# The last 64 columns of x's second half: transposing loads in place of plain loads and identity matmuls

## The chip, the cores and the metric

The kernel runs on one core of a Trainium2 chip. A core has a matrix engine (PE, TensorE), a vector engine (DVE), a scalar engine (ACT), a general engine (POOL, GpSimd) and SyncE (SP), which here only issues DMAs. Each engine runs its own instructions in order, and semaphores tie them together. Matmul results land in PSUM and are copied to SBUF by ACT or DVE. The metric is device time in microseconds of one execution.

## The reference

Two independent blocks are computed, and their outputs are put side by side. B = 1, S = 2048 positions, D = 576 channels, bf16.

```python
# A: dilated sliding-window attention, 32 heads of 18
qkv = x @ wqkv
logits[s, w] = q[s] . k[s - 2 w] * scale        # w = 0..7, masked below 0
o = softmax(logits) @ v[s - 2 w];  a = o @ wo
# B: a long convolution with gates
kv = (short 4-tap convolution of k along s) * v
y = irfft(rfft(kv) * rfft(ssm_k)) + kv * ssm_D   # causal, length S
b = q_B * y
out = concat([a, b], -1)
```

## The kernel before

**x.** The projections need x transposed: channels on partitions, positions along the row. 576 channels are four blocks of 128 and a tail of 64. `xT(kb, t0, n)` is a block's view in the large SBUF tile `xw`; `x5(jj)` is the tail of one half jj of the positions, 128 x 512, whose lower 64 partitions hold the half's first 512 positions and whose upper 64 the other 512. The first half of x is loaded as it lies (`load_x`) and transposed by PE. The second half comes by `turn_x(h)`, once for each 512 positions: a transposing DMA brings the first 512 columns straight into `xT`, and a plain DMA brings the last 64 columns as they lie into `xnat`, a view of the tile `Ks`. `transpose_tail(1)` then multiplies those 2 x 4 pieces of 128 positions with the identity on PE (L490) and copies the 128 x 512 result out of PSUM on ACT (L492).

**SP's queue.** The loads are issued from SP in program order: x, weights, k's segment 0, v's segment 0, k's segment 1, `turn_x(0)`, `turn_x(1)` (L250, L251), v's segment 1 (L219, L220), and later, as buffers come free, k's segments 2 and 3 (L210, L213), v's segments 2 and 3, and the filter's transposing loads (L227).

**The first stage** (to about 56 us). DVE runs `taps(i)`, the 4-tap convolution of the segments i = 0 to 3, each of 512 positions: multiplications L577, additions L581, and the product with v, L597. Beside it PE projects q and k. `project(comp, jj)` makes units for column blocks of 128, two halves of 512 positions each: four matmuls a half with `xT` (L378), the 64-row tails with `x5` (L389), and an ACT copy of the 128 x 1024 result (L414). L382 and L395 are the same for the last 64 columns of q or k. After each `taps(i)`, two `mirror(i, n)` units fold a segment on PE (L606) with two ACT copies (L609). `table_i` transposes sine tables on PE (L455) with two ACT copies (L459). `fold_filter(m)` folds a filter segment (L673, ACT L676).

**Order.** It is written out by hand. `units` is a list of closures for PE and ACT; `until()` runs as many of them as the next number in PLACES says (2, 14 and 13 after the first three segments' taps). Mirrors and fold units are inserted into what is left of the list at the places of AT (1, 5 and 19), where a mirror is not put between the two halves of a projection. `need(label)` runs all units up to the last one with that label; after the last segment `need("fold3")` empties the list. `early` runs a unit and advances the planner's clock for PE. PSUM tiles have two tags, "A" and "B", with two buffers each; projections, table_i and fold_filter use "A", the mirrors and `transpose_tail` use "B".

**Behind it**, `logits(hh)` multiplies q and shifted k on DVE (L832) and sums over the channels on PE (L847), two products at a time; then come softmax, the weighted sums, the output projection, the spectra (L627, L776) and the inverse transform.

Of the kernel before, what the change touches and what calls it, by code (L numbers as in the profile page):

```python
# [11 lines left out]
ACT = mybir.ActivationFunctionType  # L12
ALU = mybir.AluOpType
FP32 = mybir.dt.float32
# [39 lines left out]
def view(t, offset, dims):  # L54

    return bass.AP(tensor=t.tensor, offset=t.offset + offset, ap=[list(t.ap[0])] + [list(d) for d in dims])
# [3 lines left out]
def kernel(  # L60
# [13 lines left out]
    nc = tc.nc  # L74
# [4 lines left out]
    xf = A_x.flatten_outer_dims()  # L79
# [29 lines left out]
    pp = ctx.enter_context(tc.tile_pool(name="pp", bufs=2, space=PSUM))  # L109
# [32 lines left out]
    def x5(jj):  # L142
        return view(xw, HB * (3 + 3 * jj) + 4096, [[1, 512]])
# [39 lines left out]
    xnat = view(Ks, 4 * HB, [[HB, 4], [D, 4], [1, D]])  # L183
# [14 lines left out]
    def load_k(i):  # L198

        eng = nc.sync  # L200
        kj = sp1.tile([128, 7, D], BF16, name="kj", bufs=2)
        r0 = BL * i
        low = [(0, 64)]
        if i == 0:
            nc.gpsimd.memset(kj[0:1, 0:3, :], 0.0)
            nc.gpsimd.dma_start(kj[0:1, 3:7, :], kf[0:4, :].unsqueeze(0))
            low = [(1, 49), (49, 64)]
        for a, b in ((3, 7), (0, 3)) if i == 0 else ((0, 7),):
            for p0, p1 in low:
                eng.dma_start(kj[2 * p0:2 * p1:2, a:b], bass.AP(  # L210
                    tensor=kf.tensor, offset=kf.offset + (r0 + 4 * p0 - 3 + a) * D,
                    ap=[[4 * D, p1 - p0], [D, b - a], [1, D]]))
            eng.dma_start(kj[1:128:2, a:b], bass.AP(tensor=kf.tensor, offset=kf.offset + (r0 + 256 + 3 - a) * D,  # L213
                                                    ap=[[4 * D, 64], [-D, b - a], [1, D]]))
        kjs.append(kj)
# [24 lines left out]
    ident = main.tile([128, 128], BF16, name="ident")  # L240
# [6 lines left out]
    def turn_x(h):  # L247

        r0 = 1024 + 512 * h
        nc.sync.dma_start(xnat[:, 2 + h, :, 512:576], xf[r0:r0 + 512, 512:576].rearrange("(sb p) c -> p sb c", p=128))  # L250
        nc.sync.dma_start_transpose(view(xw, 6 * HB + 512 * h, [[1024, 4], [1, 512]]), xf[r0:r0 + 512, 0:512])  # L251

    load_k(0)
    load_w(nc.sync, 1)
    load_v(0)
    load_k(1)
    turn_x(0)
    turn_x(1)
    load_v(1)

# [61 lines left out]
    units = deque()  # L322
# [160 lines left out]
        f()  # L483
        clk["P"] += us

    def transpose_tail(jj):
        pt = pp.tile([128, 512], FP32, name="ps_x", tag="B")
        for jp in range(2):
            for sb in range(4):
                nc.tensor.matmul(pt[64 * jp:64 * jp + 64, 128 * sb:128 * sb + 128], xnat[:, 2 * jj + jp, sb, 512:576],  # L490
                                 ident[:], start=True, stop=True, tile_position=(0, 64 * jp))
        nc.scalar.activation(x5(jj), pt[:], ACT.Copy)  # L492

    def project_first(jp, ct0):

        ps = bank2("ps_proj", "A")
        for e in range(2):
            c0 = 128 * (ct0 + e)
            for kb in range(4):
                nc.tensor.matmul(ps[:, e, :], wq(kb, 0, c0, 128), xT(kb, 512 * jp, 512), start=(kb == 0), stop=False)  # L500
        for e in range(2):
            nc.tensor.matmul(ps[:, e, :], wq(4, 0, 128 * (ct0 + e), 128)[64 * jp:64 * jp + 64],
                             x5(0)[64 * jp:64 * jp + 64], start=False, stop=True, tile_position=(64 * jp, 0))
        nc.scalar.activation(view(q, S * ct0 + 512 * jp, [[S, 2], [1, 512]]), ps[:], ACT.Copy)
# [40 lines left out]
    for jj in range(2):  # L545
        if jj:
            project(0, jj)
        project(1, jj)
        if jj == 0:
            units.append((0.43, partial(early, partial(transpose_tail, 1), 0.43), "x"))  # L550
    project(0, 2)
    project(1, 2)

# [792 lines left out]
```

## Time and profile before

| | |
|---|---|
| median of 3 runs | 212.2 us (212.09 to 212.56) |
| the profiled execution | 212.5 us, of which the traced span is 210.8 |
| granted TensorE clock | 0.998 |
| PE busy | 200.1 us (95%) |
| DVE busy | 193.1 us (92%) |
| ACT busy | 150.5 us (71%) |
| POOL busy | 74.0 us (35%) |
| DMA | 39.66 MB in 35,396 packets |

An engine's busy time is a sum over stages that are limited by different things. A row of the timeline gives the start and the length of a group of like instructions; a bracket at its end gives the time for which the engine had been idle and what ended that. A row marked SPq is SP's time for issuing a DMA, not the transfer; the time to landing is told apart.

### The profile page before, as it was taken

The page shows a single profiled execution, that of the slowest core. Times are in us where ns is not written, and L with a number is a line of the kernel's source. Part 1 is how long each engine was busy: PE and PEld are TensorE (multiplying, and loading weights), DVE is VectorE, ACT ScalarE, POOL GpSimd, SP SyncE. Part 2 cuts the span into 40 slices and gives each one's busy share as a digit, 9 for nine tenths or more (in the row PEclk, how much of TensorE's full clock was granted, in tenths as well). Part 3 has the DMA queues.
Part 4 walks back from the last instruction along what each step waited for, and adds up shares of the span by engine and source line. Part 5 has one row for each costly group of instructions (what it writes and reads, how often), then busy time and mean ns, then how long its engine had stood idle before and what let it go on. Part 6 is the DMA issues. An engine that isn't in the chain of part 4 may idle for free.

```text
span 210.8 us, 5106 instructions
## 1 busy us (share of the span) xinstructions
PE 200.1 (95%) x2114; PEld 110.7 (53%) x2122; DVE 193.1 (92%) x146; ACT 150.5 (71%) x218; POOL 74.0 (35%) x111
## 2 busy tenths in 40 slices
PE   7999999999999999899999999999989999999891
PEld 2443443344554656564354666656555666666460
DVE  7989999999999999858889999999999849999981
ACT  3799988657684989986369788855666796775540
POOL 8999993001195516320175000002029004033000
PEclk9999999999999999999999999999999999999999
DMA  6999998999639336999999997587559995985133
GB/s 201 303 328 231 266 342 280 170 192 182 151 75 122 48 40 87 180 181 171 235 225 238 194 234 159 105 208 185 153 223 255 239 322 110 214 243 182 28 113 111
DMA packets 35396, 39.66 MB, mean 188 GB/s; under 512 B 17619, under 2 KB 29007, under 8 KB 35374
## 3 DMA queue, kind: packets, MB, share of 16 engines
q1 hardware_dynamic: 26812, 24.88, 47.2%
q0 software_dynamic: 6096, 11.96, 30.4%
q10 hardware_dynamic: 2466, 2.51, 3.5%
q8 instruction: 16, 0.26, 0.5%
q14 instruction: 6, 0.05, 0.1%
HBM read 13.11 MB, written 4.72 MB: 85 GB/s over the span
## 4 chain that ended last, share of the span: by engine, by line
PE 80%; ACT 10%; DVE 5%; issue 2%; DVEq 0%; ACTq 0%
PE ps_proj L378 16%; PE ps_z L1126 9%; PE ps_wo L1029 8%; PE ps_acc L973 7%; PE ps_inv L1158 7%; PE ps_fx L776 6%; PE ps_log L847 4%; PE ps_proj L500 3%; PE ps_fk L627 3%; PE ps_proj L382 3%; PE ps_proj L389 3%; ACT Ks L695 3%; PE ps_rev L673 2%; PE ps_fk L628 1%; ACT qk L977 1%
## 5 line engine op out<-in xcount | busy, mean ns | idle before, releaser
L378 PE MATMUL ps_proj<-xw 128*128 128x512 bf16 x153 | 37.4, 380 | 0.6 <-issue 0.3
L832 DVE TENSOR_TENSOR av<-qk 128x4096 bf16<-128x4096 bf16 (+1 forms) x16 | 31.7, 2013 | 2.8 <-PE ps_log L847 2.8
L378 PEld LDWEIGHTS <-xw 128*128 128x128 bf16 x160 | 14.0, 97 | 20.5 <-issue 6.2
L1099 DVE TENSOR_TENSOR qk<-xw,Ks 128x2304 bf16<-128x2304 bf16 x14 | 18.5, 1355 | 2.5 <-PE ps_inv L1158 2.4
L1139 ACT ACTIVATE av<-ps_z 128x768 bf16<-128x768 f32 x20 | 15.3, 808 | 6.2 <-PE ps_z L1126 6.2
L414 ACT ACTIVATE qk<-ps_proj 128x1024 bf16<-128x1024 f32 x14 | 14.3, 1023 | 7.6 <-PE ps_proj L389 3.3
L695 ACT ACTIVATE Ks<-ps_fk 128x576 bf16<-128x576 f32 x32 | 18.6, 717 | 1.3 <-PE ps_fk L628 1.3
L577 DVE TENSOR_TENSOR tB<-kj,skb 128x4608 bf16<-128x4608 bf16 (+1 forms) x8 | 19.3, 2417 | 0.1
L778 ACT ACTIVATE xw<-ps_fx 128x576 bf16<-128x576 f32 x32 | 18.4, 666 | 0.0
L776 PE MATMUL ps_fx<-xw,TB 128*128 128x288 bf16 x128 | 18.0, 286 | 0.2
L1055 POOL DMA_DIRECT2D Ks<-Ks x3 | 3.7, 1218 | 41.1 <-PE ps_wo L1029 28.7
L1029 PE MATMUL ps_wo<-qk 128*128 128x288 bf16 x128 | 17.8, 287 | 0.0
L627 PE MATMUL ps_fk<-Ks,TB 128*128 128x384 bf16 x62 | 16.9, 326 | 0.8 <-ACT Ks L695 0.7
L414 ACT ACTIVATE v<-ps_proj 128x1024 bf16<-128x1024 f32 x9 | 9.3, 1029 | 9.3 <-PE ps_proj L378 4.3
L973 PE MATMUL ps_acc<-av,ident 64*64 64x512 bf16 x160 | 15.3, 377 | 0.0
L628 PE MATMUL ps_fk<-Ks,TB 128*128 128x192 bf16 x62 | 15.2, 245 | 0.0
L776 PEld LDWEIGHTS <-TB 128*128 128x128 bf16 x128 | 12.0, 97 | 6.0 <-issue 2.9
L1029 PEld LDWEIGHTS <-qk 128*128 128x128 bf16 x128 | 11.6, 98 | 5.6 <-issue 3.0
L1158 PE MATMUL ps_inv<-av,TI 128*128 128x288 bf16 (+1 forms) x96 | 13.6, 293 | 0.6 <-ACT av L1139 0.6
L1161 ACT ACTIVATE v<-ps_inv 128x576 bf16<-128x576 f32 (+1 forms) x14 | 9.5, 677 | 6.3 <-PE ps_inv L1158 6.3
L977 ACT ACTIVATE qk<-ps_acc 128x1024 bf16<-128x1024 f32 x8 | 8.2, 1024 | 8.0 <-PE ps_acc L973 8.0
L956 DVE TENSOR_TENSOR av<-Ks,v 128x4096 bf16<-128x4096 bf16 x6 | 13.6, 2286 | 0.2 <-PE ps_acc L973 0.2
(199 smaller groups left out, 471.3 us busy)
## 6 DMA issues: line engine op xcount, KB each, us to landing
Ks<-Ks POOLq DMA_DIRECT2D x9, 576.0 KB, 7.1
TB<-av SPq DMA_DIRECT2D x12, 256.0 KB, 5.5
kj<-in_B_k_dram SPq DMA_DIRECT2D x6, 504.0 KB, 6.1
vt<-in_B_v_dram SPq DMA_DIRECT2D x8, 288.0 KB, 5.2
Ks<-av SPq DMA_DIRECT2D x8, 256.0 KB, 5.5
Ks<-Ks SPq DMA_DIRECT2D x3, 576.0 KB, 6.1
Ks<-in_A_x_dram SPq DMA_DIRECT2D x2, 576.0 KB, 5.2
xw<-in_A_wqkv_dram SPq DMA_DIRECT2D x2, 576.0 KB, 5.9
```

Of the source, the lines that this page charges most:

```text
L378: nc.tensor.matmul(ps[:, jp, :], wq(kb, comp, 128 * ct, 128), xT(kb, 1024 * jj + 512 * jp, 512), **se)
L414: nc.scalar.activation(view(t, o + pad + 1024 * jj, [[512, 2], [1, 512]]), ps[:], ACT.Copy)
L577: dve(2304 * n, lambda: nc.vector.tensor_tensor(to, view(kj, row * D, [[D, n], [D, 4], [1, D]]), view(skb, row * D, [[D, n], [0, 4], [1, D ...
L627: nc.tensor.matmul(o[:, 0:2], w, rhs[:, 0:2], start=start, stop=stop)
L695: nc.scalar.activation(view(Ks, k_at(m, cs ^ (m & 1)) + 96 * gi, [[768, 3], [384, 2], [1, 96]]), acc3(ps), ACT.Copy, scale=(PSG, MSG)[cs][ ...
L776: nc.tensor.matmul(ps[:, pm, 0:HD], TX[:, 2 * pm + c, 128 * gi:128 * gi + 128], kv[:, 2 * c + pm, HD * h:HD * h + HD], start=(c == 0), sto ...
L832: return P, at, step, dve(1024 * nj, lambda: nc.vector.tensor_tensor(view(P, at, [[step, 4], [256, nj], [1, 256]]), view(t, o + 256 * hh, ...
L973: nc.tensor.matmul(acc[64 * o:64 * o + 64, h, :], ident[64 * h:64 * h + 64, 64 * h:64 * h + 64], view(P, 256 * u, [[2048, 2], [1, 256]])[6 ...
L1029: nc.tensor.matmul(ps[:, r, 0:HD], oT(hh, 2 * c + r, t)[:, o:o + 128], wo[:, t // 2, t % 2, HD * h:HD * h + HD], start=(t == 0 and h == 0) ...
L1099: r = dve(3 * QTR, lambda: nc.vector.tensor_tensor(pr, view(xw, HB * XG[i] + QTR * t, [[HB, 3], [1, QTR]]), view(Ks, k_at(j - i, 0) + QTR ...
L1126: nc.tensor.matmul(view(acc[r], 512 * h, [[192, 2], [96, 2], [1, 96]])[o:o + 64], w[64 * h:64 * h + 64, 64 * h:64 * h + 64], pr[64 * h:64 ...
L1158: nc.tensor.matmul(ps[:, c, 0:n], TI[:, sl, pm, 128 * c:128 * c + 128], Y(j, pm)[:, sl, c0:c0 + n], start=(pm == 0 and sl == 0), stop=(sl ...
```

## The change

`turn_x(h)` no longer loads the last 64 columns as they lie. After the transposing load of the first 512 columns, a second transposing load brings the last 64 straight into the 64 partitions of `x5(1)` that belong to these 512 positions. `transpose_tail` goes, and with it its unit in the list. The numbers in PLACES and AT stay.

```diff
     def turn_x(h):
         r0 = 1024 + 512 * h
-        nc.sync.dma_start(xnat[:, 2 + h, :, 512:576], xf[r0:r0 + 512, 512:576].rearrange("(sb p) c -> p sb c", p=128))
         nc.sync.dma_start_transpose(view(xw, 6 * HB + 512 * h, [[1024, 4], [1, 512]]), xf[r0:r0 + 512, 0:512])
+        nc.sync.dma_start_transpose(x5(1)[64 * h:64 * h + 64], xf[r0:r0 + 512, 512:576])
...
-    def transpose_tail(jj):
-        pt = pp.tile([128, 512], FP32, name="ps_x", tag="B")
-        for jp in range(2):
-            for sb in range(4):
-                nc.tensor.matmul(pt[64 * jp:64 * jp + 64, 128 * sb:128 * sb + 128], xnat[:, 2 * jj + jp, sb, 512:576],
-                                 ident[:], start=True, stop=True, tile_position=(0, 64 * jp))
-        nc.scalar.activation(x5(jj), pt[:], ACT.Copy)
...
         project(1, jj)
-        if jj == 0:
-            units.append((0.43, partial(early, partial(transpose_tail, 1), 0.43), "x"))
```

## The prediction

> **What bounds the kernel now.** I read the page first, then the timeline of the stretch around the edit, then the waits of the vector engine, then the timeline down to where engines meet again. The first columns of a timeline row are start and length in us.
>
> ```profile
> PE 200.1 (95%) x2114; PEld 110.7 (53%) x2122; DVE 193.1 (92%) x146; ACT 150.5 (71%) x218; POOL 74.0 (35%) x111
> PE 80%; ACT 10%; DVE 5%; issue 2%; DVEq 0%; ACTq 0%
> ```
>
> PE and DVE are both nearly full, so the chain, 80% PE, names only the one that was last. What 0.4 us of PE work is worth depends on which engine sets the pace between the edit (near 30 us) and the next meeting of the two. The edit's own stretch:
>
> ```profile
> 28.62 1.04 PE L378 MATMUL ps_proj<-xw 128*128 128x512 bf16 x4
> 28.73 1.08 ACT L459 ACTIVATE TI<-ps_ti 128x512 bf16<-128x512 f32 x2 [0.36 <-PE ps_ti L455]
> 29.58 0.42 PE L490 MATMUL ps_x<-ident,Ks 128*64 128x128 bf16 x8
> 29.70 1.03 ACT L414 ACTIVATE qk<-ps_proj 128x1024 bf16<-128x1024 f32 x1
> 29.94 1.90 PE L378 MATMUL ps_proj<-xw 128*128 128x512 bf16 x7
> 30.61 0.61 ACT L492 ACTIVATE xw<-ps_x 128x512 bf16<-128x512 f32 x1
> 31.77 0.60 PE L389 MATMUL ps_proj<-xw 64*128 64x512 bf16 x4
> ```
>
> L490 and L492 are the work that goes. And this is what DVE waited for in the first 75 us, all of it:
>
> ```profile
> DVE xw L161 <- PEq L1330: 0.9, 1, 0.9
> DVE xw L577 <- DMA kj<-in_B_k_dram: 0.7, 1, 0.7
> DVE tB L173 <- issue: 0.3, 1, 0.3
> ...
> 11.88 1.36 DVE L577 TENSOR_TENSOR xw<-kj,skb 128x2304 bf16<-128x2304 bf16 x1 [0.72 <-DMA kj<-in_B_k_dram]
> ```
>
> After 11.88 us DVE waits for nobody; it runs the taps and then the logits products on its own clock. Where PE meets it:
>
> ```profile
> 63.87 2.27 DVE L832 TENSOR_TENSOR av<-qk 128x4096 bf16<-128x4096 bf16 x1
> ...
> 65.75 0.62 PE L847 MATMUL ps_log<-v,E 128*32 128x512 bf16 x8
> ...
> 66.20 0.60 PE L847 MATMUL ps_log<-av,E 128*32 128x512 bf16 x8
> ```
>
> The second half of this L847 group reads the product that DVE ends at 63.87 + 2.27 = 66.14. It starts at 66.20, 0.06 later, which is a semaphore's way: PE has no slack against DVE here. Anything that PE gains before 66.20 beyond those 0.06 us becomes waiting.
>
> **Removed from PE and ACT.** Eight matmuls at L490 and one copy at L492. PE's step from 29.58 to 29.94 is 0.36 us, the most that can leave the chain. But the projection behind it can't simply move up by 0.36. It takes one of the two buffers of tag "A". One holds the tile that ACT empties from 29.70 to 30.73; so at 29.94 it is in the other, table_i's, which ACT (L459) empties until 28.73 + 1.08 = 29.81. PE follows such a release by 0.06 (66.14 to 66.20), so it can start at 29.87: a gain of 0.07 us; the rest of L490's time only covered ACT's copy. L492's 0.61 us on ACT falls in a stretch where ACT then idles: its next instruction comes at 32.26, after 1.04 us of waiting (row below). It brings nothing by itself.
>
> **What moves.** The unit that disappears was one of those which until() pops by hand-written counts (2, 14, 13). With one fewer, the second count takes one projection half more, and mirror units, inserted at fixed places among what is left, move:
> - Segment 1's first mirror goes from in front of the third pair of projection halves to behind it. Its input is ready at 33.40 (32.04 + 1.36 of L597), its output is read only in the x spectrum, behind the logits; nothing waits on it.
> - ACT's table load at 33.31 is issued one projection's copy later. ACT waits about 1 us between such copies (1.04 in the row), so I cost it at nothing; without that cover it would be 1.28 us on ACT, not on PE, which has a second buffer.
> - Segment 2's second mirror goes from 50.6 us to behind the last key projection, right ahead of fold_filter(3). This one is tight.
>
> ```profile
> 32.26 1.02 ACT L414 ACTIVATE qk<-ps_proj 128x1024 bf16<-128x1024 f32 x1 [1.04 <-PE ps_proj L389]
> 33.31 1.28 ACT L739 ACT_TABLE_LOAD   x1
> ...
> 32.04 1.36 DVE L597 TENSOR_TENSOR xw<-xw,vt 128x2304 bf16<-128x2304 bf16 x1
> 33.32 2.55 DVE L577 TENSOR_TENSOR tB<-kj,skb 128x4608 bf16<-128x4608 bf16 x1
> ...
> 51.49 1.92 PE L382 MATMUL ps_proj<-xw 128*64 128x512 bf16 x16
> 51.58 1.19 ACT L609 ACTIVATE xw<-ps_fold 128x576 bf16<-128x576 f32 x2
> 53.45 1.02 ACT L414 ACTIVATE qk<-ps_proj 128x1024 bf16<-128x1024 f32 x1 [0.68 <-PE ps_proj L382]
> 54.53 0.41 PE L673 MATMUL ps_rev<-Ks,flip 128*128 128x288 bf16 x2 [0.28 <-ACT qk L414]
> 54.97 1.19 ACT L676 ACTIVATE Ks<-ps_rev 128x576 bf16<-128x576 f32 x2 [0.49 <-PE ps_rev L673]
> 55.67 0.41 PE L673 MATMUL ps_rev<-Ks,flip 128*128 128x288 bf16 x2 [0.25 <-ACT Ks L676]
> ```
>
> In the chain of waits the mirror and L490 stand as
>
> ```profile
> 29.65 0.35 PE ps_x L490 x8
> ...
> 50.61 0.61 PE ps_fold L606 x8
> ```
>
> Before, PE's order is mirror (0.61), key projection, fold. Afterwards the projection ends 0.61 + 0.07 earlier, so ACT copies it from 52.77 to 53.79; then come the mirror's two copies, 1.19, to 54.98; then L676's, from 54.98. Before they began at 54.97. So ACT's queue gives the same start for fold_filter(2) (55.67) to within 0.01, and if the 0.07 is not won, 0.07 later. From here to 66.20 the order of the work is that of before (need("fold3") empties the list in both kernels), so PE comes to the gate between 0.07 early and 0.07 late, against 0.06 of room. On this side the sum is 0.0 us, bounds -0.06 and +0.07.
>
> **Added: two transposing loads on SP's queue.** The rows that they change and those behind them:
>
> ```profile
> 13.72 0.62 SPq L250 DMA_DIRECT2D Ks<-in_A_x_dram  x1
> 14.76 4.76 SPq L251 DMA_TRANSPOSE xw<-in_A_x_dram  x1
> 19.57 1.26 SPq L250 DMA_DIRECT2D Ks<-in_A_x_dram  x1
> 20.88 2.21 SPq L251 DMA_TRANSPOSE xw<-in_A_x_dram  x1
> 23.14 0.60 SPq L219 DMA_DIRECT2D vt<-in_B_v_dram  x1
> ...
> 25.13 0.63 SPq L213 DMA_DIRECT2D kj<-in_B_k_dram  x1
> ...
> L213 SPq DMA_DIRECT2D kj<-in_B_k_dram x1: 627/627/627, 25.1 to 25.1; - x1
> DMA to landing us min/median/max: 6.2/6.2/6.2
> ...
> L251 SPq DMA_TRANSPOSE xw<-in_A_x_dram x2: 2215/3490/4764, 14.8 to 20.9; - x2
> ...
> DMA to landing us min/median/max: 4.5/6.4/8.3
> ...
> SPq L219 <- DVE xw L597: 2.9, 1, 2.9
> ```
>
> Behind the changed loads stand v's segment 1, then k's segment 2. The k load is the tight one: issued at 25.13, landed at 31.3, read by DVE at 33.32; it may be 2.0 us late. Anything later on SP is hidden: the last v load waits 2.9 us for DVE's L597, so up to that much delay is swallowed there.
>
> SP's cost of a 64-column transposing load is in no row. The nearest is the unobstructed 512-column one, 2.21 us; in proportion, 64/512 of it would be 0.28, the lower bound, and 2.21 itself the upper (4.76 is the row with the queue ahead still full). I take 1.0, a little above the plain issues' 0.6, since the wide row shows a transposing load dearer than those. Gone are 0.62 and 1.26. The first of these may bring nothing, since the 512-column load behind it was held up by older traffic, so the shift of the k load is 2 x 1.0 - 1.26 = +0.7 at most, 2 x 1.0 - 1.88 = +0.1 at least: inside the 2.0. The data are the same 64 KB per load as before. The tails themselves land by about 23.9 + 4.5 = 28.4 us (the second 512-column load is issued until 23.1, 0.7 later now, and the tail lands the 4.5 of the quicker transposing load after that, or a little more with its own issue) and are first read by L389 at 31.77: 3.4 us to spare. So this side is 0.0 too, with +0.5 to +1.2 if a load costs 2.21 (below).
>
> **Sum.** The profiled execution took 212.5 us, of which the span is 210.8; the median of the runs is 212.2. The change adds 0.0 (-0.06 to +0.07): I forecast 212.2. About 0.2% (0.4 us) is what can be told from no change; so even all of PE's 0.36 would only be at the edge of it.
>
> **Rivals.**
> 1. *PE's work is time.* The chain is PE from 24 us on, so its 0.36 us all arrive: 212.2 - 0.36 = 211.8. For it: 80% of the chain, and L490 stands in it. Against: the buffer at 29.81, ACT's copies until 54.98 and DVE's 66.14, three gates one after the other. All would have to be misread.
> 2. *The loads hold SP up, and DVE loses its cover* (slower). Place: DVE's L577 at 33.32 waiting for k's segment 2. It decides from 2t - 1.26 > 2.0, that is t above 1.6 us per tail load (1.9 if both savings count). At t = 2.21 the k load is 2.5 to 3.2 us late and DVE 0.5 to 1.2; DVE has no waits to give it back until 66, PE is gated by it there, so it goes to the end: 212.7 to 213.4, about 213.0. For it: the transposing rows are the dearest on SP, and two of one shape differ by a factor of two (2.21 and 4.76). Against: one tail is an eighth of the data.
> 3. *The load isn't a native transpose.* If each tail were moved element by element, 2 x 32,768 pieces would go through 16 engines. The page's main queue has 26,812 packets in 47.2% of 16 engines' 210.8 us, 59 ns each; a tenth of that for a tiny one gives 65,536 x 6 / 16 = 25 us of all engines while k is due at 33 us: about 235 us. Nothing in the trace shows it; L251 is the same kind of call with 512 columns.
>
> ```profile
> q1 hardware_dynamic: 26812, 24.88, 47.2%
> ```
>
> [...]
>
> **How the numbers follow.** Forecast (within 0.1 us) 0.55; rival 1 0.12; rival 2 0.20; rival 3 0.03; something in the new order that I don't see 0.10, of which 0.04 faster and 0.06 slower. Rival 1 ends at the bound, so half of it counts as faster and half as no change; of rival 2 the mild quarter (t just above 1.6, a few tenths late) stays within 0.2%. Faster 0.06 + 0.04 = 0.10; no change 0.55 + 0.06 + 0.05 = 0.66; slower 0.15 + 0.03 + 0.06 = 0.24. The range goes from rival 1's 211.8 to 213.0, the middle of rival 2; it leaves out that rival's dear half, the third rival and the unseen, less than 0.2 in all.
>
> **What would show it.** In the changed profile: no L490/L492 rows; PE's projection after table_i's second half starts near 29.87 with ACT's L459 as releaser; the second mirror of segment 2 behind the last key projection and L676 within 0.1 of 54.97; the second half of the L847 group at 66.2 again, now with a short wait for DVE or none; two more DMA_TRANSPOSE rows on SP of about 1.0 us. I am wrong if DVE shows a wait for kj near 33 us, if a tail row on SP exceeds 1.6 us, if PE waits for xw's tails at L389 near 31.8, or if PE passes 66.2 at a place earlier than DVE's product.

## The result: 291.0 us, against 212.2 forecast

The changed kernel takes 291.04 us in the median of 6 runs (289.6 to 292.42); the kernel before took 212.4 beside it (212.09 to 212.64). The ratio is 1.370, with a 95% interval of 1.365 to 1.375. In two kernels further down, one run that took over 1.5% longer than the fastest of its kernel does not enter the median: 217.0 us with the two wide loads, 274.64 us with 96 columns. The profiled execution took 289.72 us with a span of 288.0. The forecast was 212.2 in a range of 211.8 to 213.0, with no change the likeliest: it was wrong by 79 us.

The page of the changed kernel, with the same rows as were shown of before and the slices beside them (a digit is the busy share, or the granted clock, of 7.2 us in tenths):

```profile
PE 203.5 (71%) x2106; PEld 112.1 (39%) x2114; DVE 193.2 (67%) x146; ACT 150.1 (52%) x217; POOL 73.9 (26%) x111
PE   8999200002000019998999899999999999999983
...
DVE  8899400000000007999999958899999999699983
...
PEclk9999855555555557999999999999999999999998
DMA  7999999999999999996824899999867669979505
GB/s 229 307 255 25 3 2 2 2 64 12 2 2 2 2 118 376 229 181 148 111 44 57 129 185 184 228 227 222 197 110 202 162 209 278 294 159 236 153 24 142
...
q1 hardware_dynamic: 91324, 24.88, 87.2%
...
PE 45%; SPq 33%; DVE 7%; ACT 6%; DMA 5%; issue 2%; DVEq 0%; ACTq 0%
```

Read it from the bottom. SP's queue, which was nowhere in the chain of before, holds a third of it. The queue q1 moved the same 24.88 MB as before, in 91,324 packets instead of 26,812. That is 64,512 more: exactly 2 x 512 x 64 = 65,536 pieces of one element, less the 1,024 rows of 128 bytes that the two plain loads had been. Between 30 and 100 us PE and DVE are all but empty, while the DMA engines show nine tenths busy at mostly 2 GB/s. The work itself is what it was: DVE is busy 193.2 us (193.1 before).

SP's own timeline tells which instruction holds the queue (start and length in us):

```profile
13.67 5.64 SPq L250 DMA_TRANSPOSE xw<-in_A_x_dram  x1
19.37 1.28 SPq L251 DMA_DIRECT2D xw<-in_A_x_dram  x1
20.69 40.97 SPq L250 DMA_TRANSPOSE xw<-in_A_x_dram  x1
61.70 0.61 SPq L251 DMA_DIRECT2D xw<-in_A_x_dram  x1
62.35 39.30 SPq L219 DMA_DIRECT2D vt<-in_B_v_dram  x1
```

The two tail loads, L251, are not DMA_TRANSPOSE as the 512-column loads (here L250) are: they stand as DMA_DIRECT2D, the kind of the plain loads. Their own rows are short, 1.28 and 0.61 us. The long row is the one behind each: the second 512-column load takes 40.97 us (2.21 before), and v's segment 1 takes 39.30 (0.60 before). That is 38.8 + 38.7 = 77.5 us more on SP, about what the span grew by (77.2 us; the medians differ by 78.6). When the tails landed, and who waited:

```profile
L251 SPq DMA_DIRECT2D xw<-in_A_x_dram x2: 609/943/1277, 19.4 to 61.7; - x2
...
DMA to landing us min/median/max: 44.6/44.8/45.0
```

```profile
DVE xw L587 <- DMA vt<-in_B_v_dram: 76.2, 1, 76.2
PE ps_proj L389 <- DMA xw<-in_A_x_dram: 38.3, 1, 38.3
PE ps_proj L378 <- DMA xw<-in_A_x_dram: 35.1, 1, 35.1
```

Each tail took about 45 us to land. PE waits twice, once for each long load: 35.1 us for the columns of the second half, which were held behind the first tail, and 38.3 for the second tail itself. DVE waits once, 76.2 us, for v's segment 1 (its L587 is the L597 of before), which stood behind both. In PE's and DVE's timelines:

```profile
29.86 1.02 PE L378 MATMUL ps_proj<-xw 128*128 128x512 bf16 x4 [0.21 <-ACT TI L459]
65.95 1.44 PE L378 MATMUL ps_proj<-xw 128*128 128x512 bf16 x3 [35.07 <-DMA xw<-in_A_x_dram]
...
106.70 1.01 PE L389 MATMUL ps_proj<-xw 64*128 64x512 bf16 x3 [38.34 <-DMA xw<-in_A_x_dram]
107.64 5.72 PE L378 MATMUL ps_proj<-xw 128*128 128x512 bf16 x16
...
119.37 3.63 PE L378 MATMUL ps_proj<-xw 128*128 128x512 bf16 x16
...
108.19 1.36 DVE L587 TENSOR_TENSOR xw<-xw,vt 128x2304 bf16<-128x2304 bf16 x1 [76.22 <-DMA vt<-in_B_v_dram]
```

The same product of DVE began at 32.04 before. It comes 76.2 us later, and the span is 77.2 us longer, so nearly all of the loss is in the stretch from 30 to 108 us.

### The profile page after: what moved, and what is told of

It is laid out like the page before. It is cut to its first block, busy times and chain, and to the rows that moved or that the text cites. A ratio compares the mean times of both kernels' runs of the same rounds, so it can differ in the third digit from the quotient of the medians.

```text
span 288.0 us, 5088 instructions
## 1 busy us (share of the span) xinstructions
PE 203.5 (71%) x2106; PEld 112.1 (39%) x2114; DVE 193.2 (67%) x146; ACT 150.1 (52%) x217; POOL 73.9 (26%) x111
## 3 DMA queue, kind: packets, MB, share of 16 engines
q1 hardware_dynamic: 91324, 24.88, 87.2%
## 4 chain that ended last, share of the span: by engine, by line
PE 45%; SPq 33%; DVE 7%; ACT 6%; DMA 5%; issue 2%; DVEq 0%; ACTq 0%
SPq L250 16%; SPq L219 14%; PE ps_z L1116 7%; PE ps_wo L1019 6%; PE ps_inv L1148 5%; PE ps_acc L963 5%; PE ps_proj L378 5%; DMA kj<-in_B_k_dram 5%; PE ps_fx L766 5%; DVE tB L567 4%; DVE xw L571 3%; PE ps_log L837 3%; PE ps_fk L617 3%; ACT Ks L685 2%; PE ps_fk L618 1%
## 5 line engine op out<-in xcount | busy, mean ns | idle before, releaser
L378 PE MATMUL ps_proj<-xw 128*128 128x512 bf16 x153 | 40.0, 401 | 35.9 <-DMA xw<-in_A_x_dram 35.1
L414 ACT ACTIVATE qk<-ps_proj 128x1024 bf16<-128x1024 f32 x14 | 14.3, 1025 | 85.8 <-PE ps_proj L389 78.6
L587 DVE TENSOR_TENSOR xw<-xw,vt 128x2304 bf16<-128x2304 bf16 x4 | 5.4, 1359 | 76.3 <-DMA vt<-in_B_v_dram 76.2
L378 PEld LDWEIGHTS <-xw 128*128 128x128 bf16 x160 | 14.8, 102 | 58.3 <-issue 45.4
L389 PE MATMUL ps_proj<-xw 64*128 64x512 bf16 x40 | 7.8, 406 | 38.7 <-DMA xw<-in_A_x_dram 38.3
L726 POOL DMA_DIRECT2D Ks<-Ks x3 | 1.7, 572 | 95.7 <-DVE xw L571 87.1
L389 PEld LDWEIGHTS <-xw 64*128 64x128 bf16 x40 | 1.5, 94 | 44.6 <-issue 44.6
L1045 POOL DMA_DIRECT2D Ks<-Ks x3 | 3.6, 1217 | 41.5 <-PE ps_wo L1019 29.6
## 6 DMA issues: line engine op xcount, KB each, us to landing
vt<-in_B_v_dram SPq DMA_DIRECT2D x8, 288.0 KB, 7.8
```

The lines of the kernel that those rows point to most:

```text
L378: nc.tensor.matmul(ps[:, jp, :], wq(kb, comp, 128 * ct, 128), xT(kb, 1024 * jj + 512 * jp, 512), **se)
L414: nc.scalar.activation(view(t, o + pad + 1024 * jj, [[512, 2], [1, 512]]), ps[:], ACT.Copy)
```

## Experiments

The theory after this profile: a transposing load of 64 columns is not a transpose for the DMA engines but a plain copy of single elements; the queue works each off in about 38 us, and whatever stands behind it on SP's queue waits. The rivals: the lost cover of the removed unit or the moved mirrors (the order of the work), and the dependency of PE on the late tails.

**The loads alone.** The kernel before, matmuls and copy kept, with the two loads added; nobody reads what they bring.

```
  in turn_x(h), behind the 512-column load:
+ nc.sync.dma_start_transpose(view(Ks, (6 + h) * HB, [[1, 512]])[64:128], xf[r0:r0 + 512, 512:576])
```

> The kernel before, with the two 64-column loads of the change added behind the 512-column ones, into a place that nobody reads; matmuls, copy and order are those of before. If the loads hurt by filling the queue in front of x's last 512 positions, v and k: about 288 to 292, with DVE waiting some 76 us for v. If they hurt only because the projections wait for the tails: 213 to 216, since nothing reads them.

Measured: 290.25 us (290.15 to 290.34), ratio 1.3675, interval 1.3651 to 1.3698. SP's timeline and the waits (L252 is the added load, L250 now the plain load of the tail, L251 the 512-column load):

```profile
19.68 1.22 SPq L252 DMA_DIRECT2D Ks<-in_A_x_dram  x1
20.94 38.34 SPq L250 DMA_DIRECT2D Ks<-in_A_x_dram  x1
59.33 4.21 SPq L251 DMA_TRANSPOSE xw<-in_A_x_dram  x1
63.59 0.63 SPq L252 DMA_DIRECT2D Ks<-in_A_x_dram  x1
64.26 37.99 SPq L219 DMA_DIRECT2D vt<-in_B_v_dram  x1
```

```profile
DVE xw L598 <- DMA vt<-in_B_v_dram: 77.0, 1, 77.0
```

The whole loss is there without the rest of the change: PE's order, the mirrors and ACT are as before, and no engine reads the new tails. A plain load held behind the first tail waits 38.34 us, v's load behind the second 37.99. So what the loads hold up behind them on the queue is enough for the whole loss; a dependency on the tails is not needed for it.

**The same columns by wide loads.** The change kept, each tail brought by a 128-column load instead of a 64-column one; half of what it brings is not used. The second goes to a tile of its own.

```
+ x5b = main.tile([128, 512], BF16, name="x5b")
+ def x5h(jj, r):
+     return (x5b if (jj, r) == (1, 1) else x5(jj))[64 * r:64 * r + 64]
- nc.sync.dma_start_transpose(x5(1)[64 * h:64 * h + 64], xf[r0:r0 + 512, 512:576])
+ if h == 0:
+     nc.sync.dma_start_transpose(x5(1), bass.AP(tensor=xf.tensor,
+         offset=xf.offset + r0 * D + 512, ap=[[D, 512], [1, 128]]))
+ else:
+     nc.sync.dma_start_transpose(x5b[:], xf[r0:r0 + 512, 448:576])
  (and project reads its tails through x5h)
```

> Both tail loads 128 columns wide, the second into a new tile of its own, which nothing else uses. (The first 128-column version had put it into a part of Ks that the filter stage writes over before v's projection reads the tails: its PE waited 11.6 us there, which says nothing of the loads.) Theory 'pieces': no row over 10 us on SP, the two tail loads are DMA_TRANSPOSE; SP's queue is some 2 us later than before at k's segment 2, and DVE waits about 0.5 us for it (0.46 in the first version), so 212.4 to 212.9. Theory 'order': near 291 minus what the queue explains, at least 214.

Measured: 212.69 us (211.86 to 213.98, 11 runs) against 212.2; ratio 1.0027, interval 1.0001 to 1.0052. Its queue row and timeline, of an execution of 211.91 us:

```profile
q1 hardware_dynamic: 26844, 25.01, 47.6%
```

```profile
19.30 1.89 SPq L257 DMA_TRANSPOSE xw<-in_A_x_dram  x1
...
23.64 1.26 SPq L259 DMA_TRANSPOSE x5b<-in_A_x_dram  x1
...
26.92 0.63 SPq L218 DMA_DIRECT2D kj<-in_B_k_dram  x1
29.86 1.89 PE L386 MATMUL ps_proj<-xw 128*128 128x512 bf16 x8 [0.21 <-ACT TI L467]
33.16 2.55 DVE L575 TENSOR_TENSOR tB<-kj,skb 128x4608 bf16<-128x4608 bf16 x1
...
54.80 1.19 ACT L674 ACTIVATE Ks<-ps_rev 128x576 bf16<-128x576 f32 x2
55.50 0.41 PE L671 MATMUL ps_rev<-Ks,flip 128*128 128x288 bf16 x2 [0.85 <-ACT Ks L674]
...
66.03 0.60 PE L845 MATMUL ps_log<-av,E 128*32 128x512 bf16 x8
```

Twice the columns, and the 79 us are gone. The loads are DMA_TRANSPOSE of 1.89 and 1.26 us on SP, and q1 has 26,844 packets, 32 more than before. This kernel does what the prediction had in mind, and the next section reads these rows.

**The same, with the mirrors at their old places.** An empty unit stands where the removed one was, so the hand-written counts pop what they popped before.

```
  after project(1, jj):
+ if jj == 0:
+     units.append((0.43, partial(early, lambda: None, 0.43), "x"))
```

> The same with an empty unit where the transposing unit stood, so that all mirrors keep their places. If the moved mirrors cost nothing: equal to the one before within 0.2 us. If the prediction's reading of ACT's queue at 53 to 55 us was wrong, apart by over 0.3.

Measured: 212.53 us (211.97 to 213.91, 12 runs), ratio 1.0018, interval 0.9994 to 1.0042. With and without the moved mirrors the intervals overlap: the places of the mirrors are worth nothing that these runs can tell. In its profile, however, which is of an execution of 213.47 us, DVE does wait for k's segment 2:

```profile
27.93 0.63 SPq L218 DMA_DIRECT2D kj<-in_B_k_dram  x1
33.88 2.56 DVE L577 TENSOR_TENSOR tB<-kj,skb 128x4608 bf16<-128x4608 bf16 x1 [0.19 <-DMA kj<-in_B_k_dram]
...
66.75 0.60 PE L847 MATMUL ps_log<-av,E 128*32 128x512 bf16 x8
```

**One wide, one narrow.** The first tail by 128 columns, the second by 64, as in the change.

```
  in the wide kernel:
- nc.sync.dma_start_transpose(x5b[:], xf[r0:r0 + 512, 448:576])
+ nc.sync.dma_start_transpose(x5b[:][64:128], xf[r0:r0 + 512, 512:576])
```

> The first tail load 128 columns wide, the second 64, with a tile of its own as above. Theory 'pieces': 32,768 two-byte pieces, one stall of 36 to 39 us: 249 to 252 us.

Measured: 251.3 us (251.14 to 251.46), ratio 1.183, interval 1.177 to 1.188. Half the dose gives half the loss: +39.1 us for one narrow load, +78.6 for two.

```profile
q1 hardware_dynamic: 59084, 24.94, 69.6%
```

```profile
24.50 0.67 SPq L259 DMA_DIRECT2D x5b<-in_A_x_dram  x1
25.21 38.21 SPq L224 DMA_DIRECT2D vt<-in_B_v_dram  x1
```

The packets are 59,084 - 26,844 = 32,240 more than with both wide. That is 32,768 pieces less the packets of the wide load that they replace (some 530). With 38.21 us for them, and if the 16 engines share them evenly, a piece costs an engine 38.21 x 16 / 32,768 = 0.0187 us; this is an estimate, since no row shows a single piece.

**Ninety-six columns.** The kernel before, with one 96-column load added that nobody reads: is it the width of 64, and is the price by the piece or by the load?

```
  in turn_x(h), last:
+ if h == 1:
+     nc.sync.dma_start_transpose(view(Ks, 7 * HB, [[1, 512]])[0:96], xf[r0:r0 + 512, 480:576])
```

> The kernel before with one transposing load of 96 columns added behind the second 512-column load of x; nobody reads what it brings. If only the width below 128 decides and each 2-byte piece has its price, 512 x 96 = 49,152 pieces go through the queue: the packets of q1 grow by 49,152, the row behind the added one on SP is held 49,152 x 18.7 ns / 16 = 57 us (18.7 ns from the 38.2 us of 32,768 pieces in the kernel with one narrow load), and the time is 212.2 + 57 to 58 = 269 to 270 us. If the limit lies at or below 96 columns (or the 64 was the matter for another reason), the row is a DMA_TRANSPOSE of 1 to 2 us and the time 212 to 213.5. If the cost is a fixed one per narrow load and not per piece, the time is that of one 64-column load, 251.

Measured: 270.37 us (269.24 to 271.65, 3 runs) against 212.11; ratio 1.274, interval 1.268 to 1.280. The rows are of the execution of 274.64 us:

```profile
q1 hardware_dynamic: 75980, 24.98, 78.0%
```

```profile
23.54 0.69 SPq L253 DMA_DIRECT2D Ks<-in_A_x_dram  x1
24.28 62.77 SPq L219 DMA_DIRECT2D vt<-in_B_v_dram  x1
```

Again DMA_DIRECT2D, and 75,980 - 26,812 = 49,168 packets more, 16 beside the 49,152 pieces. One and a half times the pieces of a narrow load cost 58.3 us against 39.1, one and a half times as much. So the price goes with the pieces, and 96 columns fall on the same side as 64. The time is a little over the expectation (269 to 270). The row of 62.77 us is further over it (57), but it stems from the longer execution.

**The narrow tails later on the queue.** The change, with both narrow loads moved behind v's segment 1, k's segment 2 and v's segment 2, so that DVE's next inputs do not stand behind them.

```
  turn_x without its tail load; in the segment loop, behind load_v(i + 2):
+ if i == 0:
+     tail_loads()      # both 64-column loads of the change
```

> The two 64-column loads of the change moved in SP's queue from behind x's 512-column loads to behind v's segment 1, k's and v's segment 2. 2-byte pieces cost the same wherever they stand: PE now waits for the tails from about 31 to 105 us while DVE goes on until it needs k's segment 3 at 44 us. If queue filling alone is the loss, DVE gets 10 us further and the total falls to 278 to 285; if the wait for the tails is a loss of its own, it stays at 288 to 292.

Measured: 303.24 us (301.02 to 305.46), ratio 1.427. This missed the expectation of 278 to 292: it is worse than the change.

```profile
26.32 46.69 SPq L255 DMA_DIRECT2D xw<-in_A_x_dram  x2
73.11 40.19 SPq L210 DMA_DIRECT2D kj<-in_B_k_dram  x1
```

```profile
PE ps_proj L393 <- DMA xw<-in_A_x_dram: 85.9, 2, 46.4
DVE tB L571 <- DMA kj<-in_B_k_dram: 77.1, 1, 77.1
```

The loads start 7 us later (26.32 instead of 19.37), and PE, which needs the tails, waits 85.9 us in all instead of 73.4. DVE does get v's segment 1 and k's and v's segment 2, but then waits as long as in the change for the k load that now stands behind the tails. So DVE's wait is not what made this kernel slower than the change. These 12.5 us more of PE's wait are about what the time is longer by (303.24 against 291.04); DVE in turn waits 13.7 us for PE's logits, where it waited 2.8 in the change. So here the wait for the tails is a loss of its own. Moving the loads moves the waits; it does not hide 2 x 38 us.

**Three kernels with the second tail in Ks.** They are the wide, the wide with old places, and the one-narrow kernels, with the second tail in a part of Ks instead of a tile of its own. Later transfers write that part before v's projections read their tails there, so those wait for the transfers and work on other data.

> The change with both tail loads 128 columns wide (the first takes columns 512 to 639, that is 64 that belong to the next row, the second 448 to 575; each goes to a buffer of its own, of which the needed 64 partitions are read). Theory 'pieces' (a load of 64 columns is not transposed by the DMA hardware but moved in 2-byte pieces): these loads show as DMA_TRANSPOSE, the main queue has about 26,812 packets again, no wait of 35 us or more; 212.4 us, between 212.2 and 212.6, as the prediction's sum had it. Theory 'order' (the missing unit and the moved mirrors cost the time): stays near 291. Theory 'PE's work is time': 212.0.

> As the 128-column version, but an empty unit stands in the list where the transposing unit was, so that mirrors keep their places and only the eight matmuls and the copy are missing. If the moved mirrors cost nothing, the same as the 128-column version within 0.2 us. By the gates (buffer free at 29.81, DVE's product at 66.14) 212.35, that is 0.0 to 0.06 less than before; by 'PE's work is time' 212.0.

> The first tail load 128 columns wide, the second 64 as in the change. Theory 'pieces': 32,768 two-byte packets in place of 65,536, so about half of the 78.6 us: 251 us (246 to 256). If the partitions 64 to 127 or the first load alone were the cause, 212 or 291 instead.

Measured: 227.17, 226.41 and 265.12 us (ratios 1.069, 1.070 and 1.249). In the first, one row stands out:

```profile
PE ps_proj L395 <- DMA Ks<-Ks: 11.6, 1, 11.6
```

PE's wait of 11.6 us there is most of the 14 us or so by which each of the three lies above its counterpart with the tile (212.69, 212.53, 251.3). They say nothing of the change itself, beyond that the order of the mirrors (227.17 against 226.41) and the dose (+37.95 for one narrow load) come out alike.

## Why the prediction was wrong, step by step

**The step that failed** is the price of a tail load: t = 1.0 us, with 0.28 and 2.21 as bounds, both from rows of 512-column DMA_TRANSPOSE loads. I carried over the kind of the instruction from the kind of the call. In the program, the 64-column load is a DMA_DIRECT2D, and SP's next instruction is held 39 to 41 us behind it. No row of before was of that kind and shape, so the bounds were no bounds: they held for the two wide tails, which are DMA_TRANSPOSE (1.89 and 1.26 us). The two tails' own rows, 1.28 and 0.61 us, are near the 1.0 that I took, but that is luck: the cost stands in the row behind them, and my sign for it, a tail row over 1.6 us, did not show. The landing failed with it: I had 4.5 us, and it took 45.

**The third rival** had the mechanism, element by element, and the count, 2 x 32,768 pieces. It had two things wrong. Its chance was 0.03, because "L251 is the same kind of call", which was the same mistake again. And its piece was priced at 6 ns, a tenth of the 59 ns of a mean packet, which was a guess; the run with one narrow load gives 18.7 ns by the estimate above, so 25 us for the two loads became 77. From rows of before alone, the whole 59 ns would have given an estimate of 65,536 x 59 / 16 = 242 us, and the measured 77 lie between the two. "About 235 us" was therefore itself well short of 291.

On the width, the runs show this: the loads of 64 and of 96 columns stood as DMA_DIRECT2D and went in single elements (65,536 pieces in the changed kernel, 49,152 with 96 columns), and those of 128 and of 512 columns stood as DMA_TRANSPOSE. No transposing load of before brought fewer than 512 columns. "Nothing in the trace shows it" was therefore as true of the opposite, and I used it as a reason to set the rival aside. On SP's issue, the two wide tails took 1.89 and 1.26 us, against 0.62 and 1.26 of the plain tails that they replace.

**What the wide kernels say of the rest.** They do what I had priced, so the other terms can be read there.
- *The gain of the removed matmuls.* Predicted: PE's projection starts at 29.87, released by ACT's L459. Measured: 29.86 in the changed kernel and in the wide one (where its line is L467), after a wait of 0.21 for it. Right.
- *ACT's queue at fold_filter(3).* Predicted: L676 within 0.1 of 54.97, because the mirror's copies end at 54.98. Measured in the wide kernel: 54.80, with PE's next step at 55.50 (55.67 before). The number is nearly right, and the mirror's copies do end about there (53.55 + 1.19 = 54.74 in the wide kernel). But a second gate lies at the same time, which I did not see; that the two coincide is luck. In the kernel with the old places the mirror's copies are over by 52.83, and ACT still stands idle for 0.98 us before it starts L676 at 55.52. What moves with it is DVE (the first row is of before, the others of the kernel with the old places):

```profile
54.59 0.51 DVE L657 TENSOR_SCALAR Ks<-Ks 1x576 bf16<-1x576 bf16 x2
...
55.15 0.51 DVE L657 TENSOR_SCALAR Ks<-Ks 1x576 bf16<-1x576 bf16 x2
55.52 1.19 ACT L676 ACTIVATE Ks<-ps_rev 128x576 bf16<-128x576 f32 x2 [0.98 <-PE ps_rev L673]
56.22 0.40 PE L673 MATMUL ps_rev<-Ks,flip 128*128 128x288 bf16 x2 [0.74 <-ACT Ks L676]
```

  L657 (`negate`) comes behind DVE's last product and reads a row of Ks that L676 overwrites. From its start to that of L676 it is 0.38 us before and in the wide kernel, and 0.37 with the old places and in the changed kernel (132.21 and 132.58). No profile names DVE as the releaser, so this is inferred from the constant distance and the program. By it, DVE sets the start of fold_filter's copies with the mirror in its old place; with the mirror moved, its copies end at the same time. So the move is worth about zero.
- *The gate at 66.2.* No profile shows a wait of PE there. From PE's step behind L676 to this group it is 10.53 us in all three kernels (55.67 to 66.20, 55.50 to 66.03, 56.22 to 66.75), and PE comes 0.06, 0.17 and 0.15 us after DVE's product has ended. So by this reading PE meets DVE at 55 us, and at 66 it only arrives in step; the 0.06 that I read as a gate was what that left. Rival 2 was right that DVE's lateness goes on to there: with the old places DVE's product for segment 2 started 0.56 later than before (33.88 against 33.32), and PE came 0.55 later. A gain of PE ahead of 55 us, as in rival 1, would by this end at DVE's L657.
- *k's segment 2.* Even native, and 128 columns wide, a tail costs SP 1.26 to 1.89 us, not 1.0. The k load was issued at 26.92 and 27.93 instead of 25.13, 1.8 and 2.8 us later; against the 2.0 of room, one profile shows no wait and the other 0.19. So t, 1.6 us on average, lay around the point from which rival 2 decides, and its mechanism is there with 0.19 us, not its 0.5 to 1.2 (of the 0.56, 0.29 had been lost before: DVE's first tap waited 1.0 us for k instead of 0.7, and L597 came at 32.33 instead of 32.04).
- *The sum.* With native loads I would have forecast 212.2; the wide kernels gave 212.69 and 212.53 against 212.2; by the ratios that is +0.3% and +0.2%, one interval just above zero and one around it. No version here beats the kernel before.

What stays open: why the rows held in the changed kernel are 39 to 41 us where the others' are 38 (and the two tail rows of the kernel with the later tails take 46.69 together), and how much of the wide kernels' 0.2% to 0.3% is the late k load. The widths between 96 and 128 were not tried. Nor was a narrow load on another engine's queue: in the changed kernel no other engine issues a DMA while SP is held, so the runs do not tell whether only SP's queue is held up or all 16 DMA engines are taken.

## What to carry to other kernels

A call that looked like the one beside it compiled to something else at another shape here (DMA_DIRECT2D at 64 and 96 columns, DMA_TRANSPOSE at 128 and 512): before a DMA is priced by a neighbouring row, ask whether that row is of the same shape, and where it is not, treat another kind as a likely case, not as a remote one. A transfer in single elements showed itself here in three places at once: packets that grow by the number of elements at equal MB (91,324 instead of 26,812 at 24.88 MB), DMA engines that are nine tenths busy at 2 GB/s, and a long row (40.97 and 39.30 us) at the innocent instruction behind the load on its queue. Where 64 transposed columns are wanted, a 128-column load that fetches too much cost 1.3 to 1.9 us of the queue here, against 38.

## What the runs showed of the hardware that I had not expected

- By estimate, if the 16 DMA engines share the pieces evenly, a piece of 2 bytes cost an engine 18.7 ns (38.2 us x 16 / 32,768; 19.0 from the 58.3 us that 49,152 pieces cost). The issuing queue was held until shortly before the load landed: the first tail's own row is 1.28 us, the next one ends at 61.66, and the tail lands at about 64 (19.37 + 44.6); behind the second tail the next row ends at 101.65, and PE, which waits for that tail, goes on at 106.70.
- PE's granted clock fell while PE idled, and it came back late. PE stops at 30.88 us; the granted clock is 1.00 until 33 us, 0.71 in the next and 0.50 from 34 on, also during the four matmuls that PE does from 65.95. PE takes up work again at 106.70, the granted clock is 0.50 until 111 us and 1.00 from 112 on, and the 16 matmuls of 128x512 at 107.64 took 5.72 us where those at 119.37 took 3.63. By this comparison the pause cost PE about 2 us more after it ended; the return took about 5 us here.
